# Four memsets at the front of a queue, and five queues ordered anew behind the first key products

## The chip, the cores and the metric

The kernel runs on one core of a Trainium2 chip. A core has a matrix engine (TensorE, PE in the profile; its weight loads are shown as PEld), a vector engine (VectorE, DVE), a scalar engine (ScalarE, ACT), GpSimd (POOL) and SyncE (SP), which here issues nearly all DMAs. Each engine works through its own queue in order, and the queues are tied together by semaphores. The metric is the device time of one execution in microseconds (us), the median of the runs.

## The reference

The input x has 2048 rows of 448 bf16 values. One transformer block is computed: a layer norm, linear attention with 16 heads of 28 dimensions, a residual, a second layer norm, a gated feed-forward part of width 1792, and a second residual. Cut to what matters:

```python
q, k, v = split(layernorm(x) @ wqkv)              # 16 heads of 28
phi_q = concat([softmax(q @ w_phi), softmax(-(q @ w_phi))])
phi_k = concat([softmax(k @ w_phi), softmax(-(k @ w_phi))])
kv  = einsum("bhsf,bhsd->bhfd", phi_k, v)         # sums over all 2048 rows
z   = phi_k.sum over the rows
num = einsum("bhqf,bhfd->bhqd", phi_q, kv)
den = einsum("bhqf,bhf->bhq", phi_q, z) + 1e-6
h   = x + (num / den) @ wo
g, u = layernorm(h) @ w_gate, layernorm(h) @ w_up
out = h + (sigmoid(g) * u) @ w_down
```

No query can be finished before kv and z have been summed over all rows.

## The kernel before

The 2048 rows are 16 tiles of 128 rows, numbered 0 to 15. An operation is created with a name, a list of engines that may run it, and the buffers that it reads and writes. From the buffers a class named Graph works out who has to wait for whom. The table ORDER (from line 210) is written out by hand or by a planner. It lists every operation's name in one of five queues, and so says which engine runs it and in which sequence. Nothing is reordered later: what stands behind a waiting operation waits too. The profile knows lines of the code and not names. A name is found in the trace by counting along its queue: the ninth xn of the tiles that DVE and the other engines run is xn8, and so on.

The stages and the names, with their lines:

- **First layer norm**, per tile t: x*t* loads the rows (L397); bst*t* and agg*t* are its statistics on DVE (L503, L504). For a group of tiles, ve1 and nm1 (L511, L514) prepare variance and mean, pow1 (L516, POOL alone) takes the inverse root, and nb1 (L520, POOL) the bias. The last group holds tiles 12 to 15, so ve1_12, nm1_12, pow1_12 and nb1_12 serve four tiles, and need agg15, whose rows x14 brings. xn*t* writes the normalised tile to one of three buffers (L529 on ACT, L532 on DVE or POOL). xT*t* transposes it: on PE for the first four tiles, else as a DMA issued by SP (L542). So xn8 can't start before xT5 has landed, nor xn7 before xT4.
- **Weights**: ld_k, ld_v and ld_q (L461, transposing DMAs) bring the parts of wqkv; w2m0 and w2m1 (L571) multiply them by w_phi, and w2e copies the product out of PSUM. ld_wo, ld_wg, ld_wu and ld_wd load the later weights with L397, 56 KB to 448 KB each.
- **Keys and values**, per tile: pva and pvb are the products of keys and values (L298, all paired matmuls of 64 rows share this line), ek takes both exponentials (L630, L631, ACT), ss their sums (L634, DVE), rs the reciprocals (L640, DVE), and phi the normalised features (L644; POOL for most tiles, DVE for tiles 10 and 15). phi has three buffers and ek and ss have five. v1 copies the values (L489). kva and kvb (L298) add the tile's share of kv to two PSUM banks, which seed (L666) has started with the 1e-6: a small product of two tiles epsl and epsr. These are filled by the four memsets epsl0 and epsr0 (L409, L410, L413, L414; two each), on POOL. After kvb15, kvzA to kvzD (L709 on DVE, L713 on ACT) mask the sums into a table, and kvzones puts its ones there (L434).
- **Queries**: pqa and pqb (L298) of four tiles and a quarter pair of heads, eq their exponentials (L680, L681, ACT). num*t* (L298) multiplies by the table; rsm, qq, b, c and rden (L740 to L748, DVE) combine the two halves, and o (L752, DVE or POOL) divides. oT transposes (PE for tiles 0 and 1, with the copies oT0e and oT1e, else a DMA). num*t* and num*t+1* use the same two banks: the next num waits for c of the one before.
- **Second norm**: woa and wob (L298) are the output products; h (L771 on ACT, L774 on DVE) adds the residual; nm (L777), sq (L779, ACT), ve (L782), pow2 (L784, POOL alone) and hn (L788) normalise; hT transposes (PE for tiles 0 and 1, with the copies hT0e and hT1e on DVE, else a DMA).
- **Feed-forward**: ga and gb (L298) are gate and up for a slice of 128 columns, sig (L847, ACT) and hh (L848, DVE) combine them. dn, dp, dm, dl (L298, L875) are the down products, fin (L882) the last residual, out the store. The name of a piece says the first tile and the slice: ga0_1 is slice 1 of tiles 0 and 1. Four banks serve gate and up, so a pair of slices waits for hh of the pair before.

The profile's critical chain and the queues meet in the first 80 us; from there on PE has hardly any idle time.

Of the kernel before, what the change touches and what calls it, by code (L numbers as in the profile page):

```python
# [208 lines left out]

ORDER = {  # L210
    "sp": (
        "x1 x0 ld_k0 x2 ld_k2 x4 x6 ld_v0 x10 ld_v2 x8 ld_q2 ld_q1 ld_q0 x12 ld_q3 xT4 xT5 x14 xT6 xT7 xT8 xT9 "
        "xT10 xT11 xT12 xT13 xT14 xT15 ld_wg0 ld_wu1 ld_wu3 ld_wd1 ld_wg1 ld_woe0 ld_wu0 ld_woe1 ld_woo0 ld_woo1 "
        "ld_wg3 ld_wg2 ld_wd6 ld_wd2 ld_wd3 ld_wd5 ld_wd0 ld_wu2 oT2 oT3 oT5 oT4 oT6 oT7 ld_wd4 hT3 hT2 oT8 oT9 "
        "hT4 hT5 hT6 hT7 oT11 oT10 oT12 out3 out1 hT9 hT8 oT13 hT11 hT10 oT14 oT15 out0 out5 hT12 hT14 out2 hT15 "
        "out4 hT13 out10 out7 out8 out9 out6 out11 out13 out12 out14 out15 out15b "
    ),
    "act": (
        "wphi3 wphi2 wphi1 wphi0 wTe0 wTe1 xT1e xT0e wTe2 w2e0_0 w2e0_1 w2e0_2 w2e0_3 xn3 xn4 ek0 ek1 xn5 v1_0 "
        "v1_1 xn6 ek2 v1_2 v1_3 ek3 w2e1_1 ek4 v1_4 ek5 v1_5 w2e1_0 v1_6 ek6 xn11 ek7 v1_7 xn12 ek8 xn13 ek9 "  # L220
        "w2e1_3 w2e1_2 ek10 xn14 ek11 xn15 v1_11 ek12 eq0_0 ek13 ek14 ek15 v1_14 eq0_1 kvzB eq1_0 eq1_1 eq2_0 oT0e "
        "eq2_1 h1 h0 sq1 sq0 eq3_0 eq3_1 sig0_1 sig0_0 sig0_3 sig0_2 sig0_5 sig0_4 sq2 sig0_7 sig0_6 sq3 sig0_9 "
        "sig0_8 sq5 sig0_11 sig0_10 sig0_13 sig0_12 sig2_1 sig2_0 sq4 sig2_3 sig2_2 sq7 sq6 sig2_5 sig2_4 sig2_6 "
        "sig2_7 sig2_8 sig2_9 sig2_10 sig2_11 sig2_12 sig2_13 sig4_1 sq9 sig4_0 sig4_3 sq8 sig4_2 sig4_5 sig4_4 "
        "sig4_7 sig4_6 sig4_9 sq10 sig4_8 sq11 sig4_11 sig4_10 sig4_13 sig4_12 sig8_1 sig8_0 sq13 sig8_2 sig8_3 "
        "sig8_4 sig8_5 sq12 sig8_6 sq14 sq15 sig8_7 sig8_9 sig8_8 sig8_10 sig8_11 sig8_13 sig8_12 sig12_0 sig12_1 "
        "sig12_3 sig12_2 sig12_5 sig12_4 sig12_7 sig12_6 sig12_9 sig12_8 sig12_11 sig12_10 sig12_12 sig12_13 "
    ),
    "pe": (
        "warm0 warm1 warm2 wT0 wT1 xT1 warm3 xT0 warm4 warm5 wT2 w2m0_0 wT3 warm6 w2m0_1 w2m0_2 warm7 w2m0_3 warm8 "  # L230
        "ppa0 warm9 ppb0 vva0 xT3 xT2 vvb0 ppa2 ppb2 vva2 vvb2 w2m1_1 w2m1_0 seed kva0 pva4 kvb0 pvb4 pva5 kva1 "
        "pvb5 kvb1 pva6 kva2 pvb6 pva7 w2m1_2 w2m1_3 pvb7 pva8 kvb2 kva3 pvb8 kvb3 pva9 kva4 pvb9 kvb4 pva10 kva5 "
        "pvb10 pva11 kvb5 kva6 pvb11 pqa0_0 pva12 kvb6 kva7 pvb12 kvb7 pqb0_0 kva8 pva13 kvb8 kva9 pvb13 kvb9 "
        "kva10 pva14 pvb14 kvb10 pva15 kva11 pvb15 pqa0_1 kvb11 kva12 pqb0_1 pqa1_0 kvb12 kva13 kvb13 kva14 kvb14 "
        "kva15 kvb15 pqb1_0 pqa1_1 num0 num1 pqb1_1 pqa2_0 num2 pqb2_0 pqa2_1 oT0 oT1 pqb2_1 num3 woa0 wob0 num4 "
        "pqa3_0 pqb3_0 num5 pqa3_1 pqb3_1 hT1 hT0 num6 ga0_1 ga0_0 gb0_1 gb0_0 num7 woa2 ga0_3 ga0_2 gb0_3 gb0_2 "
        "wob2 ga0_5 ga0_4 gb0_5 gb0_4 num8 woa4 ga0_7 ga0_6 gb0_7 gb0_6 wob4 num9 ga0_9 ga0_8 gb0_9 gb0_8 woa6 "
        "ga0_11 ga0_10 gb0_11 gb0_10 wob6 ga0_13 ga0_12 gb0_13 gb0_12 dn0_0 dn0_4 ga2_1 ga2_0 gb2_1 gb2_0 dn0_8 "
        "dn0_11 ga2_3 ga2_2 gb2_3 num10 gb2_2 dp0_0 dp0_4 ga2_5 ga2_4 gb2_5 gb2_4 dp0_8 dp0_11 ga2_6 ga2_7 gb2_6 "
        "gb2_7 woa8 ga2_8 ga2_9 gb2_8 gb2_9 wob8 num11 ga2_10 ga2_11 gb2_10 gb2_11 dn2_0 ga2_12 ga2_13 gb2_12 "  # L240
        "gb2_13 dn2_4 dn2_8 ga4_1 num12 gb4_1 ga4_0 dn2_11 gb4_0 dp2_0 ga4_3 ga4_2 gb4_3 dp2_4 num13 gb4_2 ga4_5 "
# [707 lines left out]
```

## Time and profile before

The median of three runs is 205.43 us (205.39 to 205.56). The profiled execution took 205.5 us, 203.7 us of them between its first and its last instruction. The TensorE clock is granted in full (1.000).

| stretch, us | PE busy | DVE busy | ACT busy | POOL busy | DMA share |
|---|---|---|---|---|---|
| 0 to 10 | 8.62 | 6.88 | 5.73 | 5.20 | 0.88 |
| 10 to 20 | 9.44 | 9.67 | 8.89 | 9.52 | 0.62 |
| 20 to 30 | 9.31 | 10.00 | 9.40 | 8.05 | 0.40 |
| 30 to 40 | 9.93 | 10.00 | 9.21 | 9.22 | 0.46 |
| 40 to 50 | 9.81 | 8.24 | 8.26 | 4.30 | 1.06 |
| 50 to 60 | 9.64 | 9.25 | 9.29 | 4.30 | 0.55 |
| 60 to 70 | 9.56 | 8.95 | 4.39 | 4.44 | 0.25 |
| 70 to 80 | 9.96 | 8.78 | 4.14 | 1.09 | 0.39 |

Busy times are microseconds out of the ten of the stretch. PE's matmuls are pipelined, so a busy PE may still be waiting inside a group; the DMA share is that of 16 DMA engines. Over the span PE is busy for 197.6 us, DVE for 135.9, ACT for 96.5 and POOL for 56.8.

### The profile page before, as it was taken

Reading aid. Unit: us, or ns where it says so; the run is one execution under the profiler, and the core shown is the slowest. Engines: PE = TensorE matmul, PEld = TensorE weight load, DVE = VectorE, ACT = ScalarE, POOL = GpSimd, SP = SyncE. Lnnn points to the kernel's source line nnn. Section 1 sums busy time; section 2 is a strip of 40 time slices with the busy share of each in tenths; the row PEclk is TensorE's granted clock in tenths of the full one; section 3 lists DMA queues with packets and bytes.
Section 4 is the critical chain, followed back from the end, with each engine's and each line's share of the span. In section 5 each row is a group of like instructions: output and inputs, shape, how many; then the busy total and the mean of one; then the engine's idle time right before and its main releaser. Section 6 shows DMA issues by size and latency. Waiting matters only on the chain.

```text
span 203.7 us, 5832 instructions
## 1 busy us (share of the span) xinstructions
PE 197.6 (97%) x2476; PEld 109.8 (54%) x2476; DVE 135.9 (67%) x329; ACT 96.5 (47%) x194; POOL 56.8 (28%) x98
## 2 busy tenths in 40 slices
PE   7999989999989999999999999999999999999995
PEld 2744545565547876777444544444555555544443
DVE  5899999988988888667667967526532422262224
ACT  2998999879893544522333343323522222222220
POOL 4599699861064320500023020001400000000000
DMA  6965332899622351230004411030212000004002
GB/s 151 318 140 122 55 80 55 245 309 345 196 52 55 65 89 28 55 81 0 3 0 80 122 29 26 3 74 24 58 40 56 3 0 3 0 0 138 0 0 90
DMA packets 32866, 16.25 MB, mean 80 GB/s; under 512 B 25096, under 2 KB 31944, under 8 KB 32840
## 3 DMA queue, kind: packets, MB, share of 16 engines
q1 hardware_dynamic: 32336, 15.86, 30.5%
q8 instruction: 19, 0.31, 0.7%
q10 hardware_dynamic: 504, 0.03, 0.2%
q14 instruction: 7, 0.06, 0.1%
HBM read 8.34 MB, written 1.84 MB: 50 GB/s over the span
## 4 chain that ended last, share of the span: by engine, by line
PE 78%; DVE 9%; POOL 4%; DMA 3%; ACT 2%; issue 1%; SPq 1%; POOLq 0%
PE psum L298 73%; PE psum L875 5%; DMA x_sb<-in_A_x_dram 3%; DVE c_sb L746 1%; DVE b_sb L743 1%; POOL rst L516 1%; DVE st L503 1%; DVE xn_pad L532 1%; DVE ss L634 1%; POOL phi L644 1%; DVE rsm L740 1%; ACT xn_pad L529 1%; SPq L397 1%; DVE o_pad L752 1%; ACT v L489 0%
## 5 line engine op out<-in xcount | busy, mean ns | idle before, releaser
L298 PE MATMUL psum<-xnT,wg_sb 64*128 64x512 bf16 (+1 forms) x490 | 93.3, 333 | 0.4 <-DVE rsm L740 0.3
L298 PE MATMUL psum<-xnT,wu_sb 64*128 64x512 bf16 (+1 forms) x490 | 93.2, 333 | 0.0
L847 ACT ACTIVATE sg_sb<-psum 128x512 bf16<-128x512 f32 (+1 forms) x70 | 35.0, 511 | 91.2 <-PE psum L298 90.7
L848 DVE SCALAR_TENSOR_TENSOR hhT<-sg_sb,psum 128x512 bf16<-128x512 bf16 (+1 forms) x70 | 38.9, 576 | 53.9 <-ACT sg_sb L847 53.2
L298 PEld LDWEIGHTS psum<-xnT,wg_sb 64*128 64x128 bf16 x490 | 44.4, 94 | 23.8 <-DVE hhT L848 4.7
L298 PEld LDWEIGHTS psum<-xnT,wu_sb 64*128 64x128 bf16 x490 | 44.4, 94 | 13.4
L298 PE MATMUL psum<-wd_sb,hhT 64*128 64x448 bf16 x336 | 36.8, 349 | 0.0
L298 PEld LDWEIGHTS psum<-wd_sb,hhT 64*128 64x128 bf16 x336 | 17.2, 94 | 15.0 <-DVE x_sb L774 0.6
L644 POOL TENSOR_TENSOR phi<-hhT,rs 128x896 bf16<-128x896 bf16 x14 | 23.3, 1688 | 2.4 <-DVE rs L640 1.9
L298 PE MATMUL psum<-Wk,xnT 64*128 64x448 bf16 x112 | 22.5, 350 | 0.5 <-ACT Wk L489 0.2
L298 PE MATMUL psum<-wv_sb,xnT 64*128 64x448 bf16 x112 | 22.5, 351 | 0.1
L782 POOL TENSOR_SCALAR ve<-ssq 128x1 f32<-128x1 f32 x14 | 3.0, 212 | 65.2 <-ACT junk L779 65.0
L634 DVE TENSOR_REDUCE ss<-hhT 128x32 f32<-128x896 bf16 x16 | 16.9, 1059 | 0.1
L298 PE MATMUL psum<-xnT,Wq 64*120 64x512 bf16 x112 | 14.7, 384 | 0.1
L298 PE MATMUL psum<-wo_o,oT 64*128 64x448 bf16 x56 | 13.2, 349 | 0.0
L298 PE MATMUL psum<-wo_e,oT 64*128 64x448 bf16 x56 | 13.1, 349 | 0.0
L875 PE MATMUL psum<-wd_sb,hhT 128*128 128x448 bf16 (+2 forms) x70 | 11.2, 316 | 0.0
L882 DVE SCALAR_TENSOR_TENSOR x_sb<-psum,x_sb 128x448 bf16<-128x448 f32 (+2 forms) x17 | 9.4, 592 | 2.2 <-PE psum L875 1.6
L779 ACT ACTIVATE junk<-x_sb,sum 128x448 bf16<-128x448 bf16 x16 | 10.5, 658 | 0.0
L503 DVE BATCH_NORM_STATS2 st<-x_sb 128x6 f32<-128x448 bf16 x16 | 9.4, 607 | 1.7 <-DMA x_sb<-in_A_x_dram 1.6
L298 PEld LDWEIGHTS psum<-Wk,xnT 64*128 64x128 bf16 x112 | 7.6, 94 | 5.4 <-PE psum L298 0.5
L746 DVE TENSOR_TENSOR c_sb<-b_sb,psum 128x464 bf16<-128x464 bf16 x16 | 10.1, 633 | 0.4
(93 smaller groups left out, 237.0 us busy)
## 6 DMA issues: line engine op xcount, KB each, us to landing
out_dram<-x_sb SPq DMA_DIRECT2D x15, 112.0 KB, 1.8
x_sb<-in_A_x_dram SPq DMA_DIRECT2D x7, 224.0 KB, 4.6
wd_sb<-in_B_w_down_dram SPq DMA_DIRECT2D x7, 224.0 KB, 9.7
wg_sb<-in_B_w_gate_dram SPq DMA_DIRECT2D x3, 448.0 KB, 8.8
wu_sb<-in_B_w_up_dram SPq DMA_DIRECT2D x3, 448.0 KB, 7.3
wv_sb<-in_A_wqkv_dram SPq DMA_DIRECT2D x2, 224.0 KB, 4.8
...
```

What stands on the lines that cost most here:

```text
L298: p = e.matmul(o, lhsT=w, rhs=r, start=st, stop=sp, tile_position=(row, 0))
L397: return op(eng, name, lambda e: e.dma_start(dst, src), r=r, w=w, dma="in" if eng == "sp" else "ain", nring=48 if eng == "sp" else 8, kb=kb)
L503: op("dve", "bst%d" % t, lambda e: e.bn_stats(st1[:, t, :], x_sb[:, t, :]), r=[("x", t)], w=[("st1", t)])
L634: op("dve", "ss%d" % t, lambda e: e.tensor_reduce(ss[:, s, :].rearrange("p (b h) -> p b h", h=2), eks.rearrange("p b (d h) -> p b h d", h= ...
L644: return e.tensor_tensor(phi[:, sp, :, :, :].rearrange("p b a n -> p (b a) n")[:, :, 0:56].rearrange("p b (d h) -> p b d h", h=2), eks.rea ...
L746: op("dve", "c%d" % t, lambda e: e.tensor_tensor(h3(c_sb), h3(b_sb), OPv[:, :, :, 0:EV], ALU.add), r=K("b") + BB, w=K("c"))
L779: op("act", "sq%d" % t, lambda e: e.activation(junk[:, t % 2, :], h_sb[:, t, :], ACT.Square, bias=sum2[:, t:t + 1], scale=-float(D), accum ...
L782: op(("pool", "dve"), "ve%d" % t, lambda e: e.tensor_scalar(ve2[:, t:t + 1], ssq2[:, t:t + 1], 1.0 / D ** 3, EPS, op0=ALU.mult, op1=ALU.ad ...
L847: op("act", "sig" + nm, lambda e: e.activation(sg_sb[:, k, 0:N], bk(bg)[:, 0:N], ACT.Tanh, scale=0.5), r=[B(bg)], w=[("sg", k)])
L848: op("dve", "hh" + nm, lambda e: e.scalar_tensor_tensor(out=hhT[(t0 // 4) % NHH][:, ff, ns], in0=sg_sb[:, k, 0:N], scalar=1.0, in1=bk(bu)[ ...
L875: p = e.matmul(bk(b)[:, lo:hi], lhsT=hb[:, ff, TS(t)], rhs=wd_sb[:, ff, lo:hi], start=ff == 0, stop=ff == FT - 1)
L882: op("dve", "fin%d%s" % (t, nm), lambda e: e.scalar_tensor_tensor(out=h_sb[:, t, lo:hi], in0=bk(b)[:, lo:hi], scalar=0.5, in1=h_sb[:, t, l ...
```

## The change

Only ORDER changes. epsl0 and epsr0 move on POOL from behind ve1_8 and v1ones to just behind wqpad, ahead of nm1_1. From the first key products on, all five queues have another sequence, up to about the place where the first down products (dn0_0) stand on PE; behind that the queues are the same. The operations, their buffers and their waits on each other are the same too. Some operations change the engine: xn5 goes from ACT to POOL; kvzones, kvzA and kvzC from DVE to ACT and kvzB from ACT to DVE; v1_15 to ACT and v1_14 to DVE; o1, o2, hn1, hn2, hn3, ve0 and ve1, nm2, nm3 and nm5 from DVE to POOL; o4, o6, o7, hn0, ve2, ve3, ve5, nm0 and nm1 from POOL to DVE; oT0e and oT1e change places; of the small group operations ve1_12, nm1_6 and nm1_8 go to POOL, and nm1_12, ve1_6 and ve1_8 to DVE. On SP, loads of later weights are put between the first loads and transposes. The core of the diff:

```diff
     "sp": (
-        "x1 x0 ld_k0 x2 ld_k2 x4 x6 ld_v0 x10 ld_v2 x8 ld_q2 ld_q1 ld_q0 x12 ld_q3 xT4 xT5 x14 xT6 xT7 xT8 xT9 "
-        "xT10 xT11 xT12 xT13 xT14 xT15 ld_wg0 ld_wu1 ld_wu3 ld_wd1 ld_wg1 ld_woe0 ld_wu0 ld_woe1 ld_woo0 ld_woo1 "
-        "ld_wg3 ld_wg2 ld_wd6 ld_wd2 ld_wd3 ld_wd5 ld_wd0 ld_wu2 oT2 oT3 oT5 oT4 oT6 oT7 ld_wd4 hT3 hT2 oT8 oT9 "
+        "x1 x0 ld_k0 x2 ld_k2 x4 x6 ld_v0 x10 ld_v2 x8 ld_woe1 ld_wu0 ld_q2 ld_q1 ld_q0 x12 ld_woo1 ld_q3 xT4 xT5 "
+        "x14 xT6 ld_wd0 xT7 xT8 ld_wd6 xT9 xT10 xT11 ld_wu2 xT12 xT13 ld_wu1 ld_wd5 xT14 xT15 ld_woo0 ld_wg0 "
+        "ld_wg1 ld_wg2 ld_wg3 ld_woe0 ld_wu3 oT3 ld_wd3 oT2 ld_wd2 oT5 oT4 oT6 ld_wd4 oT7 hT2 ld_wd1 hT3 oT8 oT9 "
...
     "act": (
-        "wphi3 wphi2 wphi1 wphi0 wTe0 wTe1 xT1e xT0e wTe2 w2e0_0 w2e0_1 w2e0_2 w2e0_3 xn3 xn4 ek0 ek1 xn5 v1_0 "
...
-        "w2e1_3 w2e1_2 ek10 xn14 ek11 xn15 v1_11 ek12 eq0_0 ek13 ek14 ek15 v1_14 eq0_1 kvzB eq1_0 eq1_1 eq2_0 oT0e "
+        "wphi3 wphi2 wphi1 wphi0 wTe0 wTe1 xT1e xT0e wTe2 w2e0_0 w2e0_1 w2e0_2 w2e0_3 xn3 xn4 ek0 ek1 v1_0 v1_1 "
...
+        "w2e1_2 w2e1_3 ek10 ek11 xn15 v1_11 ek12 eq0_0 ek13 kvzones ek14 ek15 v1_15 eq0_1 kvzA kvzC eq1_0 eq1_1 "
...
     "pe": (
...
-        "ppa0 warm9 ppb0 vva0 xT3 xT2 vvb0 ppa2 ppb2 vva2 vvb2 w2m1_1 w2m1_0 seed kva0 pva4 kvb0 pvb4 pva5 kva1 "
...
-        "kva10 pva14 pvb14 kvb10 pva15 kva11 pvb15 pqa0_1 kvb11 kva12 pqb0_1 pqa1_0 kvb12 kva13 kvb13 kva14 kvb14 "
-        "kva15 kvb15 pqb1_0 pqa1_1 num0 num1 pqb1_1 pqa2_0 num2 pqb2_0 pqa2_1 oT0 oT1 pqb2_1 num3 woa0 wob0 num4 "
-        "pqa3_0 pqb3_0 num5 pqa3_1 pqb3_1 hT1 hT0 num6 ga0_1 ga0_0 gb0_1 gb0_0 num7 woa2 ga0_3 ga0_2 gb0_3 gb0_2 "
...
+        "ppa0 warm9 ppb0 vva0 xT3 xT2 vvb0 ppa2 ppb2 vva2 vvb2 w2m1_1 seed w2m1_0 pva4 kva0 pvb4 kvb0 pva5 kva1 "
...
+        "kvb9 kva10 pvb14 kvb10 kva11 pva15 kvb11 pvb15 kva12 pqa0_1 kvb12 pqb0_1 kva13 pqa1_0 kvb13 kva14 kvb14 "
         "kva15 kvb15 pqb1_0 pqa1_1 num0 num1 pqb1_1 pqa2_0 num2 pqb2_0 pqa2_1 oT0 oT1 pqb2_1 num3 woa0 wob0 num4 "
-        "pqa3_0 pqb3_0 num5 pqa3_1 pqb3_1 hT1 hT0 num6 ga0_1 ga0_0 gb0_1 gb0_0 num7 woa2 ga0_3 ga0_2 gb0_3 gb0_2 "
+        "pqa3_0 pqb3_0 num5 pqa3_1 pqb3_1 hT1 num6 hT0 ga0_1 ga0_0 gb0_1 num7 gb0_0 woa2 ga0_3 ga0_2 gb0_3 gb0_2 "
...
     "dve": (
...
-        "bst10 agg11 bst9 bst7 agg6 agg7 agg9 bst8 agg8 agg10 mask2 xT3e xT2e ss0 nm1_8 nm1_6 rs0 ss1 bst13 rs1 "
-        "bst12 ss2 bst14 rs2 agg14 xn8 ss3 agg13 agg12 rs3 xn9 bst15 ss4 agg15 xn10 ve1_12 ss5 rs4 ss6 rs5 ss7 rs6 "
-        "v1_8 ss8 v1_9 rs7 ss9 rs8 v1_10 ss10 rs9 rs10 kvzones ss11 v1_12 rs11 phi10 ss12 v1_13 rs12 ss13 rs13 "
-        "ss14 rs14 v1_15 ss15 rs15 phi15 kvzC kvzD kvzA rsm0 qq0 rsm1 b0 qq1 c0 b1 rden0 c1 rsm2 rden1 qq2 o1 b2 "
-        "c2 oT1e rden2 rsm3 qq3 b3 c3 o2 rden3 rsm4 qq4 b4 c4 ve1 rsm5 qq5 ve0 hn1 rden4 b5 c5 hT1e hT0e rsm6 qq6 "
...
+        "bst6 bst8 mask2 agg6 agg10 agg8 agg7 bst11 ve1_6 bst9 agg11 xT3e xT2e agg9 ve1_8 ss0 rs0 ss1 bst13 bst12 "
+        "rs1 ss2 bst14 rs2 xn8 ss3 rs3 agg13 agg14 xn9 bst15 ss4 xn10 agg12 agg15 ss5 nm1_12 rs4 ss6 rs5 ss7 v1_8 "
+        "rs6 v1_9 rs7 ss8 rs8 ss9 v1_10 rs9 ss10 ss11 v1_12 rs10 rs11 phi10 ss12 rs12 v1_13 ss13 rs13 ss14 rs14 "
+        "v1_14 ss15 rs15 phi15 kvzB kvzD rsm0 qq0 rsm1 b0 qq1 c0 b1 rden0 c1 rden1 rsm2 qq2 b2 c2 oT0e rsm3 qq3 b3 "
+        "c3 rden3 rden2 rsm4 qq4 b4 c4 nm0 nm1 rsm5 qq5 b5 c5 hn0 hT1e rsm6 rden5 qq6 hT0e b6 c6 rden4 o4 rden6 "
...
     "pool": (
-        "neghalf ident0 ident phipad wqpad nm1_1 pow1_1 ve1_0 pow1_0 nm1_2 ve1_2 ve1_3 pow1_3 nm1_3 pow1_2 nb1_3 "
-        "ve1_4 nm1_4 pow1_4 nb1_4 nb1_2 xn2 opad0 ve1_6 pow1_6 ve1_8 v1ones epsl0 epsr0 pow1_8 nb1_6 phi0 nb1_8 "
-        "xn7 phi1 phi2 phi3 nm1_12 pow1_12 nb1_12 phi4 phi5 phi6 phi7 phi8 phi9 phi11 phi12 phi13 phi14 o0 nm1 o3 "
-        "pow2_1 nm0 pow2_0 hn0 o5 o4 o6 o7 ve2 pow2_2 ve3 pow2_3 ve5 ve4 pow2_4 pow2_5 ve7 pow2_7 ve6 pow2_6 ve8 "
...
+        "neghalf ident0 ident phipad wqpad epsl0 epsr0 nm1_1 pow1_1 ve1_0 pow1_0 nm1_2 ve1_2 ve1_3 pow1_3 v1ones "
+        "nm1_3 pow1_2 nb1_3 ve1_4 nm1_4 pow1_4 nb1_4 nb1_2 opad0 xn2 nm1_6 pow1_6 xn5 nm1_8 pow1_8 nb1_6 nb1_8 "
+        "phi0 xn7 phi1 phi2 phi3 ve1_12 pow1_12 nb1_12 phi4 phi5 phi6 phi7 phi8 phi9 phi11 phi12 phi13 phi14 o0 o1 "
+        "o3 o2 ve1 pow2_1 ve0 hn1 pow2_0 o5 nm2 pow2_2 nm3 pow2_3 hn2 hn3 ve4 nm5 pow2_4 pow2_5 ve7 pow2_7 ve6 "
...
```

## The prediction

> **What bounds the kernel now.** I read the page's busy shares first, then the waits and the chain, then the timelines of VectorE and GpSimd around the first wait. PE is the bound:
>
> ```profile
> PE 197.6 (97%) x2476; PEld 109.8 (54%) x2476; DVE 135.9 (67%) x329; ACT 96.5 (47%) x194; POOL 56.8 (28%) x98
> ```
>
> Its matmuls are neither more nor fewer after the change, so only PE's stalls can move. From 77 us on (dn0_0) the queues are unchanged and PE hardly waits: what it has lost or won by then stays. The waits from 14 to 30 us, and those from 46 to 62 us:
>
> ```profile
> PEld psum L298 <- POOL phi L644: 1.0, 1, 1.0
> PE psum L298 <- POOL phi L644: 0.6, 1, 0.6
> DVE st L503 <- DMA x_sb<-in_A_x_dram: 0.2, 1, 0.2
> ...
> PEld psum L298 <- DVE c_sb L746: 1.7, 4, 0.6
> PEld psum L298 <- ACT eq L681: 1.0, 3, 0.4
> ```
>
> In the first stretch PE waits once, for phi4. In the second it waits in small pieces for VectorE's c and ScalarE's eq. The chain shows why phi4 is late: x14's rows, statistics, pow1_12, nb1_12, phi4.
>
> ```profile
> 15.92 2.94 DMA x_sb<-in_A_x_dram
> ...
> 19.80 2.07 DVE xn_pad L532
> ...
> 25.56 1.04 POOL rst L516
> ...
> 26.89 1.70 POOL phi L644
> 28.59 0.05 issue
> 28.64 0.97 PE psum L298 x22
> ```
>
> And the timelines of VectorE (three lines) and GpSimd (two):
>
> ```profile
> 19.72 2.16 DVE L532 TENSOR_SCALAR xn_pad<-x_sb,nm,rst 128x512 bf16<-128x512 bf16 x1
> 23.19 0.31 DVE L532 TENSOR_SCALAR xn_pad<-x_sb,nm,rst 128x512 bf16<-128x512 bf16 x1
> 34.44 0.81 DVE L434 CAST kvz<-mask 128x24 bf16<-128x24 f32 x1
> ...
> 18.40 3.33 POOL L644 TENSOR_TENSOR phi<-hhT,rs 128x896 bf16<-128x896 bf16 x2
> 23.34 1.70 POOL L644 TENSOR_TENSOR phi<-hhT,rs 128x896 bf16<-128x896 bf16 x1 [1.62 <-DVE rs L640]
> ```
>
> xn8 (19.72) took 2.16 and ended at 21.88, just behind phi2 (end 21.72). xn9, the same work, started 0.15 ahead of phi3 and took 0.31. kvzones, 24 numbers per partition, took 0.81 and ended 0.08 behind phi8. So a VectorE instruction of these forms that meets a running phi stands still until it ends.
>
> **The change, part by part.** The profiled execution took 205.5 us (203.7 span, 1.8 around it), 0.07 over the median 205.43; durations come from it and the sum is added to the median.
>
> *Memsets.* They ran from 13.98 to 14.73, 0.75 us. In front, GpSimd is idle from 2.00 to 3.72 waiting for agg1, so they cost 0. The room goes to xn5 (0.76, until now ScalarE's at 0.83). v1ones and opad0 (0.45 and 0.35) now stand ahead of xn2 and push its end from 12.34 to about 12.7; xT2 on PE starts at 12.98, which hides it. Without that cover it would be 0.3. By the same rows phi0 starts at 15.86 (15.83 before).
>
> *Loads on SP.* ld_woe1, ld_wu0 and ld_woo1 (560 KB) now stand ahead of xT4. Their issue is three rows of about 0.47, 1.4 us. The stretches 7 to 9 us moved 374 and 384 GB/s, so the data is 1.5 us. xT4 was issued at 12.19, when xn4 was ready, behind an issue that ended at 11.66: it would go at about 13.2. xT4 itself feeds xn7 at 17.66 with 2 us to spare; x14, behind xT5, has 0. Bounds for x14's landing: 0, since the DMA share was 0.06 and 0.09 in the stretches 13 to 14 and 15 to 16 and could take the data in; +1.0, if xT4, xT5 and x14 all move with the issue. I take +0.5. The other loads moved forward (0.43 to 0.6 to issue each) stand between transposes that waited for xn, except ld_wd1, below. The 16 MB are the same, so the full DMAs of 38 to 53 us only become less full; nobody waited there.
>
> *xn8 and xn9.* The new order puts bst12 ahead of rs1, so phi1 ends at 19.9 (20.08 before), and x14 0.5 later puts rs2's end at 20.25. xn8 stands right behind rs2, phi2 needs a semaphore more: xn8 comes first and takes 0.4, a gain of 1.75. But then phi2 runs to about 22.05, when rs3 is already done (20.25 + xn8 0.35 + ss3 1.0 + rs3 0.3 = 21.9), phi3 follows without a gap, and xn9, which agg13 and agg14 now hold back by 0.16, meets it: it ends at about 23.9 instead of 23.49. The block has moved, not gone. ss4 starts at 24.3 (23.95), agg15, now behind xn10, ends at 25.8 (25.10), and the 1.84 of nm or ve, pow1_12 and nb1_12 put phi4 at 27.6 (26.89): +0.7. Bounds: -1.0 with neither blocked, +1.7 with both (x14 on time and xn9 0.16 too late).
>
> The Trainium skill, SBUF — State Buffer, Who interferes with whom, says that VectorE's two-port modes and GpSimd share one pair of ports as a lock, that whoever issues first holds it for a whole instruction, and that the other blocks fully. xn8 (2.16) and xn9 (0.31) agree; by that rule xn9 is blocked whenever phi3 goes first, and the sum is the forecast's, or with xn8 blocked as well that of the second rival.
>
> *From phi4 to kvb15.* phi4 to phi9 follow each other at 1.67: phi9 ends at 37.65 (36.91). The gaps behind it (0.44 for kvb8, 0.28 for rs12, in front of which v1_13 stood) shrink, but rs13 now comes behind v1_13 (0.53): phi10 to 38.2, ss12 and rs12 to 39.45, phi12 at 39.5, v1_13, ss13 and rs13 to 41.25, phi13 to 43.0, phi14 to 44.65, phi15 and the last pair 45.95 against 45.56: +0.4. PE saves 0.26 (pva10's wait), 0.23 (pva14 and pvb14 no longer in a row: 0.98 against 0.75) and 0.23 (kva13, kvb13); that is hidden behind the phi chain. kvzones leaves VectorE (0.68 there), which is hidden too while phi10 waits for phi9. Bounds: -1.1 and +1.7.
>
> *Masks and eq.* ScalarE had kvzB (0.60) ahead of eq1_0; now kvzA and kvzC, 1.15. eq1_0 would start 0.35 later, and pqa2_0 began 0.05 after eq1_0's end: +0.35 there. oT1 now waits for o1 on GpSimd, behind o0 (0.94): 51.95 against 51.57. num3 is 0.23 later, woa0 0.15, sq0's end 0.17, since VectorE no longer has o1 and o2 (0.66, 0.62).
>
> *hT0e.* GpSimd gets hn1 (0.77) ahead of pow2_0, which ends at 59.75 instead of 59.13; hn0, now VectorE's at 0.40, ends at 60.25 instead of 60.01. rsm6, rden5 and qq6, 0.45 by their starts, now stand ahead of hT0e: it ends at 61.35 instead of 60.92, and ga0_1 with it. This +0.43 includes the paragraph above. Bounds: 0.2, if PE fills it with num6, and 0.6.
>
> *61 to 77 us.* num9 fills the 0.20 that PE waited behind wob6 (0.77 against 0.57); num8 no longer stands ahead of woa4, and ga0_7 waits 0.12 for hh0_5: -0.08. Bounds -0.4 and +0.2.
>
> *ld_wd1.* It was issued at 37.58. Now it stands behind hT2, which waits for hn2, on GpSimd behind pow2_3: hn2 ends at 73.5, hT2's issue takes 1.2, and ld_wd4, of the same size, landed in 2.80: 77.6. All of this moves by the same 0.4 of the phi chain; dn0_0 without it would stand at 77.06 + 0.43 - 0.08 = 77.4. So +0.2; bounds 0 and +0.6. hT3 behind it lands at about 77.8 to 79.1, ga2_1 needs it at 79.
>
> Sum: 0.40 + 0.43 - 0.08 + 0.20 = +0.95: 205.43 + 0.95 = **206.4**.
>
> **Rivals.**
> 1. *Faster: neither xn is blocked.* Place: the seam between phi2 and phi3. It decides if phi2 ends before rs3's semaphore, by less than 0.15 in my times; kvzones got through such a seam, 0.06 wide, between phi8 and phi9. Then VectorE is 1.6 sooner at ss4, phi4 starts a us earlier and PE's wait (0.59 and the 0.26 behind it) goes, with the 0.46 of split pairs: kvb15 -1.1. With +0.43 - 0.08 and ld_wd1 at 0: 204.7. Against it: phi1 and phi2 left no seam for xn8.
> 2. *Slower by more: one block more.* Either x14 is not late and both xn8 and xn9 stand (+1.7 at phi4), or phi10 loses to phi11. For: before, phi10 started at 36.91, as phi9 ended, and only because phi11 still waited for kvb8 (37.20); PE now reaches kvb8 within 0.2 of phi9's end. If phi11 goes first, ss12 and all behind it wait 1.69, of which the gaps give 0.3 back: 206.4 + 1.4 = 207.8.
> 3. *No change to be told.* x14 is on time, xn9 still slips in, and PE's regained 0.7 covers eq1_0 and hT0e: 205.4. For: PE's stalls before are only 0.2 to 0.6 each. Against: hT0e's added rows lie on no cover.
>
> **Numbers.** 0.2%, 0.41 us, is about what a measurement of this kernel can tell from no change. The forecast has 0.45 (its own range 205.9 to 207.0), rival 1 0.22, rival 2 0.20, rival 3 0.13. So faster 0.22, same 0.13, slower 0.65. The range 204.8 to 207.9 leaves out about a third of rival 1 and of rival 2.
>
> **What would show it.** Four memsets ahead of 3 us. xn8 at 0.3 to 0.4 and xn9 at 1.7 to 2.1 (rival 1: both short; rival 2: both long, or phi10 starting 1.7 behind phi9). PE's wait for phi4 at 29.3. eq1_0 about 0.35 later against kvb15; hT0e behind qq6; ga0_1 near 61.9; a wait of dn0_0 for a wd load. The forecast is wrong if the x loads land as early as before, or if VectorE finds a seam at phi3.

## The result and the profile after

The changed kernel takes 207.61 us (median of 4 runs, 207.49 to 208.11) against 205.41 for the kernel before on the same chip: a ratio of 1.0123, 95% interval 1.0104 to 1.0141. Ratios here are estimates from the runs within 1.5% of the fastest of their kernel, with a 95% interval, and not quotients of the medians. The forecast was 206.4 in a range of 204.8 to 207.9. The sign was right, the size less than half. The profiled execution took 207.59 us (205.8 span), so it stands for the median.

Line numbers of the changed kernel are two higher than those of the kernel before (L298 is L300). The page's line of busy times of the changed kernel:

```profile
PE 197.2 (96%) x2476; PEld 111.8 (54%) x2476; DVE 134.0 (65%) x326; ACT 96.3 (47%) x196; POOL 57.8 (28%) x100
```

PE works as long as before (197.6) in a span that is 2.1 us longer: the loss is one or more stalls of PE. Who waited for whom between 60 and 82 us (total, times, longest):

```profile
PE psum L300 <- DMA wd_sb<-in_B_w_down_dram: 1.9, 1, 1.9
...
PE psum L300 <- DVE xnT L491: 0.9, 1, 0.9
```

The first line is new, and as long as nearly the whole loss. PE's longest wait in the same stretch before, weight loads (PEld) aside, was:

```profile
PE psum L298 <- DVE rsm L740: 0.3, 1, 0.3
```

The changed kernel's chain, in order of time (start, length, what):

```profile
45.20 0.60 ACT kvz L715 x2
45.81 0.60 ACT kvz L715 x2
46.44 1.02 ACT eq L682
...
72.27 1.52 POOL hn_pad L790 x2
73.79 0.46 SPq L797
74.29 4.59 DMA wd_sb<-in_B_w_down_dram
78.88 0.25 issue
79.13 49.61 PE psum L300 x658
```

SP stands at hT2 until hn2 is done on GpSimd (73.03), issues its transposes for 1.19 us, then ld_wd1 at 74.29. The load needs 4.59 us to land, and dn0_0 starts at 79.13 (77.06 before). The work in front of it on PE, gb0_12, starts at 76.73 in both traces. From dn0_0 on everything is 2.05 to 2.08 later, to the last matmul. So all that happens ahead of dn0_0 sums to nothing here, and ld_wd1 alone makes the loss.

What travelled while the load was on its way, by DMA queue (packets, MB, share of the engines' time) and with the median time to landing of what was issued:

```profile
q14 instruction: 1, 0.01, 2.7%
q8 instruction: 1, 0.02, 1.3%
...
wd_sb<-in_B_w_down_dram SPq DMA_DIRECT2D x1, 224.0 KB, 4.6
```

q8 brings instructions, 16,384 bytes at a time; such a packet runs about every 250 records of PE. Here it ran at 77.04, with 8,192 bytes of q14 beside it at 77.08. The load's 896-byte packets had all moved by 77.04, yet it counts as landed only at 78.88. Packets of 4 bytes, called completions here, close a transfer (16 of them this load, in the trace of e7 below). Twelve such packets started between 76.9 and 77.2 and all ended at 78.76 to 78.77, after 1.58 to 1.85 us. The profile doesn't say which of them are the load's and which are those of hT3 behind it.

The first stretch shows another order than the forecast's. Waits of the changed kernel from 14 to 30 us, then the timelines of VectorE (three lines) and GpSimd (one):

```profile
DVE st L505 <- DMA x_sb<-in_A_x_dram: 1.1, 1, 1.1
POOL phi L646 <- PE psum L300: 1.1, 1, 1.1
...
PEld psum L300 <- POOL phi L646: 0.5, 2, 0.3
```

```profile
20.14 0.63 DVE L505 BATCH_NORM_STATS2 st<-x_sb 128x6 f32<-128x448 bf16 x1 [1.11 <-DMA x_sb<-in_A_x_dram]
20.93 0.32 DVE L534 TENSOR_SCALAR xn_pad<-x_sb,nm,rst 128x512 bf16<-128x512 bf16 x1
22.65 0.38 DVE L534 TENSOR_SCALAR xn_pad<-x_sb,nm,rst 128x512 bf16<-128x512 bf16 x1
...
21.09 3.48 POOL L646 TENSOR_TENSOR phi<-hhT,rs 128x896 bf16<-128x896 bf16 x2 [1.06 <-PE psum L300]
```

x14 landed at 20.11 (18.86 before); bst14 waited 1.11 for it. xn8 (0.32, before 2.16) started while GpSimd was idle, 0.16 ahead of phi2. xn9 came up 0.14 before phi2's end at 22.79 and slipped in between phi2 and phi3. phi4 started at 26.78 (26.89), kvb15 0.40 earlier than before.

Then this was given back. Waits of the changed kernel from 46 to 62 us:

```profile
PEld psum L300 <- ACT eq L683: 1.3, 2, 1.0
...
PEld psum L300 <- DVE c_sb L748: 0.8, 2, 0.6
PE psum L300 <- ACT eq L683: 0.6, 1, 0.6
```

eq1_0 started 1.28 behind kvb15's end (0.72 before), behind kvzA and kvzC: the first three lines of the chain above. hT0e ended at 61.01 (60.92) and ga0_1 started at 61.37 (61.13), 0.24 later than before.

### The profile page after: what moved, and what is told of

The parts are those of the page before. It is cut to its first block, busy times and chain, and to the rows that moved or that the text cites. A ratio compares the mean times of both kernels' runs of the same rounds, so it can differ in the third digit from the quotient of the medians.

```text
span 205.8 us, 5832 instructions
## 1 busy us (share of the span) xinstructions
PE 197.2 (96%) x2476; PEld 111.8 (54%) x2476; DVE 134.0 (65%) x326; ACT 96.3 (47%) x196; POOL 57.8 (28%) x100
## 4 chain that ended last, share of the span: by engine, by line
PE 82%; POOL 5%; DVE 4%; DMA 3%; ACT 3%; issue 1%; SPq 0%; DVEq 0%; POOLq 0%
PE psum L300 76%; PE psum L877 5%; DMA wd_sb<-in_B_w_down_dram 2%; POOL rst L518 1%; POOL hn_pad L790 1%; DVE st L505 1%; DMA x_sb<-in_A_x_dram 1%; POOL phi L646 1%; POOL rst L786 1%; PE psum L573 1%; ACT kvz L715 1%; ACT eq L682 0%; ACT eq L683 0%; ACT hhT L633 0%; ACT hhT L632 0%
## 5 line engine op out<-in xcount | busy, mean ns | idle before, releaser
L300 PE MATMUL psum<-xnT,wg_sb 64*128 64x512 bf16 (+1 forms) x490 | 93.4, 333 | 1.0 <-DVE xnT L491 0.9
L300 PE MATMUL psum<-xnT,wu_sb 64*128 64x512 bf16 (+1 forms) x490 | 93.1, 333 | 0.0
L300 PEld LDWEIGHTS psum<-xnT,wg_sb 64*128 64x128 bf16 x490 | 44.3, 94 | 23.4 <-DVE hhT L850 4.7
L300 PEld LDWEIGHTS psum<-xnT,wu_sb 64*128 64x128 bf16 x490 | 44.3, 94 | 12.9
L300 PE MATMUL psum<-wd_sb,hhT 64*128 64x448 bf16 x336 | 36.9, 349 | 1.9 <-DMA wd_sb<-in_B_w_down_dram 1.9
L300 PEld LDWEIGHTS psum<-wd_sb,hhT 64*128 64x128 bf16 x336 | 17.6, 94 | 16.7 <-DVE hhT L850 2.1
L300 PE MATMUL psum<-Wk,xnT 64*128 64x448 bf16 x112 | 22.6, 351 | 0.7 <-ACT Wk L491 0.5
L300 PE MATMUL psum<-wv_sb,xnT 64*128 64x448 bf16 x112 | 22.7, 351 | 0.1
L300 PE MATMUL psum<-xnT,Wq 64*120 64x512 bf16 x112 | 14.9, 385 | 0.7 <-ACT eq L683 0.6
L300 PE MATMUL psum<-wo_o,oT 64*128 64x448 bf16 x56 | 13.2, 349 | 0.0
L300 PE MATMUL psum<-wo_e,oT 64*128 64x448 bf16 x56 | 13.1, 349 | 0.0
L300 PEld LDWEIGHTS psum<-Wk,xnT 64*128 64x128 bf16 x112 | 7.5, 94 | 6.6 <-ACT v L491 0.8
```

The source lines that it names most:

```text
L300: p = e.matmul(o, lhsT=w, rhs=r, start=st, stop=sp, tile_position=(row, 0))
```

## The experiments

Every time has beside it the kernel before on the same chip, 205.37 to 205.42 in the first three sets of runs, 205.59 and 205.41 in the last two; ratios are against it.

### Is ld_wd1 all of the loss?

Two kernels: the changed one with ld_wd1 early, and the one before with ld_wd1 late.

```diff
 e1_wd1_early (the changed kernel, "sp")
-... oT7 hT2 ld_wd1 hT3 ...
+... ld_wu3 ld_wd1 oT3 ...
 e2_before_wd1_late (the kernel before, "sp")
-... ld_wu3 ld_wd1 ld_wg1 ...
+... hT3 ld_wd1 hT2 ...
```

> The changed kernel with ld_wd1 alone moved back to the end of the weight loads (behind ld_wu3, issued near 41 us). Theory A: the whole loss of 2.07 us is dn0_0's wait for ld_wd1, since PE stood at 76.73 in both kernels just ahead of dn0_0. Then 205.5 us, the same as before within 0.2, and dn0_0 at 77.06. Rival B: hT3 is late next (it landed at 80.29, 0.35 ahead of ga2_1), so that a wait of ga2_1 takes the place: 206.0 to 207.0.

> The kernel before with ld_wd1 alone moved back, between hT3 and hT2. Theory A: the place of this one load costs the time by itself. hT3's issue ended at 73.91, so ld_wd1 goes at 73.95; at ld_wd4's 2.80 to landing dn0_0 (77.06) would not wait, 205.4; at the 4.59 that it took in the changed kernel it lands at 78.5 and the time is 206.9. If 205.4 comes out, the landing is not long of itself and the late issue (74.29 and behind hT2) is what counts.

e1 took 205.24 us (10 runs, ratio 1.0006, 0.9986 to 1.0026): the whole loss is gone, and with it any gain or loss of the rest that could be told. dn0_0 started at 76.62. e2 took 206.45 (ratio 1.0048, 1.0030 to 1.0067): this load alone, late, costs the kernel before 1.0 us. There it was issued at 73.98, landed after 3.93 us, and dn0_0 started at 78.16 instead of 77.06. The 0.3 us by which it was earlier and the 0.7 us by which it landed faster than in the changed kernel are the difference between the two losses.

The place in the queue decides already by one step:

```diff
 e7_wd1_ahead_hT2 (the changed kernel, "sp")
-... oT7 hT2 ld_wd1 hT3 ...
+... oT7 ld_wd1 hT2 hT3 ...
```

> The changed kernel with ld_wd1 moved by one place only, ahead of hT2 (behind oT7), instead of behind it. Theory A (the loss is that ld_wd1 stands behind hT2, which waits for hn2 until 73 us): it is issued near 71 and lands between 73.5 and 76, dn0_0 does not wait for it and starts at 76.6 to 77.1, time 205.2 to 205.5: all of the loss gone by one place. Theory B (what counts is that the load is among the last 16-engine transfers at 75 to 77 us, where packets stand for 1 to 1.8 us; wherever it stands late, something needed behind it pays): dn0_0 or the ga2 products wait for it or for hT2, hT3, time 206 or more.

205.37 us (ratio 1.0000, 0.9985 to 1.0015). Theory A: the load went out at 70.60, since it no longer waited for hn2, and had landed at 73.34.

```profile
q1 hardware_dynamic: 820, 0.36, 47.6%
...
wd_sb<-in_B_w_down_dram SPq DMA_DIRECT2D x1, 224.0 KB, 2.7
```

These are the queues and the load between 70.5 and 73.4 us of that kernel. No instruction packet ran, and the load landed in 2.74.

### Why did the load take 4.59 us to land?

First suspect: hT3's transposes, which follow it and whose 256-byte packets stood together with those completions.

```diff
 e10_hT3_behind_oT8 (the changed kernel, "sp")
-... hT2 ld_wd1 hT3 oT8 oT9 ...
+... hT2 ld_wd1 oT8 hT3 oT9 ...
```

> The changed kernel with nothing but hT3's transposes moved from behind ld_wd1 to behind oT8, so that ld_wd1 still waits behind hT2 but shares the DMA engines with no transpose that follows it. Read at ld_wd1 and dn0_0, not at the end time, since hT3 now comes late for ga2_1 (it should land near 81.5, some 2.5 us after ga2_1 needs it). Theory A (the last 1.6 to 1.8 us of ld_wd1's landing belong to hT3's transposes, whose small packets stood together with the load's): it lands in 2.7 to 3.0 instead of 4.59, that is near 77.2, and dn0_0 starts at 77.2 to 77.5 instead of 79.13. Theory B (they belong to the load itself, or to the 16 KB instruction fetch that ran at 77.0): it lands after 4.3 to 4.7 again and dn0_0 starts at 78.8 to 79.2.

The load took 4.38 us with no transpose behind it before oT8 was issued at 78.70; dn0_0 started at 79.72, 0.24 behind the landing. (The end, 209.61 us, is later still because hT3 came late, as meant.) So it isn't hT3. The queues of this kernel from 75 to 79.5 us:

```profile
GB/s 73 243 291 282 232 43 1 0 0 0 0 24 64 104 72 225 215 327 358 303 263 88 16 73 0 0 8 8 8 8 16 8 8 16 24 24 0 0 0 0
...
q8 instruction: 1, 0.02, 1.8%
q14 instruction: 1, 0.01, 0.7%
...
wd_sb<-in_B_w_down_dram SPq DMA_DIRECT2D x1, 224.0 KB, 4.4
```

The row of GB/s has 40 slices of 0.11 us. The bulk of the load is through by 77.6; a thin tail of 8 to 24 GB/s follows until 79.1. In the packets this tail is 16 of the load's 256, and the 16 KB instruction packet had run from 76.71 to 78.02. That suggested the fetch. Over the 24 late loads of this size in the traces taken (ld_wd4 and ld_wd1), the landing sorts by it:

| a 16 KB instruction packet | loads | time to landing, us |
|---|---|---|
| none between issue and landing | 10 | 2.71 to 2.87; once 3.26, beside an 8 KB packet (e16, below); beside another one (e3) 2.86 |
| running when the load was issued | 3 | 3.38 to 3.59 |
| began between issue and landing | 11 | 3.69 to 4.73 |

Of the eleven, only ld_wd1 in the changed kernel and in e10 had an 8 KB packet beside it as well, so that packet doesn't make the difference. A coincidence in time is not yet a cause, so the fetch was moved, with all orders left alone: more and shorter warm-up matmuls on zeros at the head of PE's queue let it come so many instructions earlier.

```diff
 e14_fetch_moved_away (the changed kernel), e15_wd1_ahead_fetch_into (e7)
-for i, (n, size) in enumerate(((9, 512), (1, 128), ...
+for i, (n, size) in enumerate(((89, 32), (1, 128), ...
```

> The changed kernel, its orders as they are, with warm0 as 89 matmuls of 32 columns on zeros instead of 9 of 512, so that TensorE's queue has 160 instructions more (80 matmuls, 80 weight loads) ahead of all else and its 16,384-byte instruction fetch, which came at 77.04 on the changed kernel's trace, comes about 160 instructions earlier in the order: by the trace at 72.8 to 73.9, ahead of ld_wd1's packets. Theory A (the fetch shares a DMA engine with the load and holds that engine's rows and what queues behind them): ld_wd1 lands in 2.7 to 3.4 instead of 4.59, dn0_0 starts at 77.1 to 77.6 instead of 79.13, time 205.6 to 206.0 instead of 207.6, which is the loss the forecast had for this term. Theory B (the landing is long for another reason, such as being queued behind hT2's transposes, and the fetch only happened beside it): 4.3 to 4.7 again, dn0_0 at 79, time 207.5.

> The seventh experiment (ld_wd1 ahead of hT2, landed in 2.74, 205.37) with the same 80 matmuls more in warm0. The fetch that came at 75.81 there should come near 71.5 to 72.5, among ld_wd1's packets (71.75 to 73.0 there). Theory A: ld_wd1 now lands in 3.7 to 4.7, at 74.3 to 75.3, still ahead of dn0_0, so the time stays within 0.3 of 205.4; that also prices the added matmuls themselves, which stand in the first 6 us, at nothing. Theory B: 2.7 to 2.9 as before. If the time moves by more than 0.3 the added matmuls cost something of their own, and the time of the run beside this one has to be read less that.

Both landings moved the way theory A has it. In e14 the load was issued at 74.94 behind the same hT2, and these are the queues from 74.9 to 77.9 us:

```profile
q1 hardware_dynamic: 1351, 0.49, 71.8%
...
wd_sb<-in_B_w_down_dram SPq DMA_DIRECT2D x1, 224.0 KB, 2.9
```

2.87 instead of 4.59. In e15 the fetch ran at 72.47, as the load was issued (72.62), and it took 3.59 instead of 2.74, 0.74 of these 0.85 in its issue (1.31 instead of 0.57). That a fetch lengthens the time from issue to landing is therefore shown in both directions. But the time of e14 did not fall: 208.32 us (ratio 1.0144, 1.0114 to 1.0173). The fetch came at 71.35, earlier than expected, onto oT7's transposes. The queues of e14 from 70.2 to 74.5 us, and what PE waited for from 70 to 80:

```profile
q8 instruction: 1, 0.02, 2.3%
...
oT<-o_pad SPq DMA_TRANSPOSE x1, 4.1
```

```profile
PEld psum L300 <- DMA oT<-o_pad: 1.6, 1, 1.6
PE psum L300 <- DMA oT<-o_pad: 1.3, 1, 1.3
```

oT7 landed after 4.14 us (2.31 in the changed kernel), woa6 waited for it, and dn0_0 started at 79.07 though the load had been there since 77.81. e15 took 208.19 (ratio 1.0143), 2.8 us above e7: its fetch held oT7 too (landed 75.06), and its kvb15 was 2.0 later, 0.8 of it already at phi4. So the added matmuls are not free, as that expectation had allowed for, and the end times of e14 and e15 don't price the fetch alone. A third place was tried:

```diff
 e16_fetch_between (the changed kernel)
-for i, (n, size) in enumerate(((9, 512), (1, 128), ...
+for i, (n, size) in enumerate(((57, 80), (1, 128), ...
```

> The changed kernel, its orders as they are, with warm0 as 57 matmuls of 80 columns (about as many columns as 9 of 512): 96 instructions more on TensorE instead of the 160 of the fourteenth kernel, so that the fetch should fall between two transfers that TensorE waits for, behind oT7 (landed 71.94 on the changed kernel's trace) and ahead of ld_wd1's packets (75.5 to 77.0), at 72.5 to 74.5. Theory A (the whole loss of the changed kernel is that a fetch meets a transfer which lands last before TensorE needs it): ld_wd1 lands in 2.7 to 3.4, woa6 does not wait for oT7, dn0_0 starts at 77.1 to 77.7, time 205.6 to 206.2, with not one instruction in another order. Theory B (there is always something late enough to be hit in this order, or the landing is not the cause of the loss): dn0_0 at 78.5 to 79.2, time 207 or more.

208.5 us (206.4 to 210.56, ratio 1.0108, 1.0072 to 1.0144): theory B, with dn0_0 at 80.33, later than either theory had it. The profile is of the run of 208.75. The fetch came at 75.07 and met hT2. SP's timeline of this kernel:

```profile
74.67 2.11 SPq L797 DMA_TRANSPOSE xnT<-hn_pad  x1
76.82 0.58 SPq L399 DMA_DIRECT2D wd_sb<-in_B_w_down_dram  x1
```

The transposes' issue took 2.11 instead of 1.19, and ld_wd1 behind it landed at 80.08. In this profile xn9 was held as well (1.34 us); phi4 came 0.8 later and kvb15 1.8. What is shown, then: where the added matmuls moved the fetch onto a transfer, its landing grew by 0.85 (the load in e15) to 1.8 us (oT7 in e14). That the changed order with the fetch between all late transfers would run at 205.7 is not shown; in this order oT7, hT2 and ld_wd1 follow each other so closely that each place tried hit one of them.

### The front of GpSimd's queue, and VectorE's seams

The memsets alone:

```diff
 e3_memsets_only (the kernel before, "pool")
-neghalf ident0 ident phipad wqpad nm1_1 ... v1ones epsl0 epsr0 pow1_8 ...
+neghalf ident0 ident phipad wqpad epsl0 epsr0 nm1_1 ... v1ones pow1_8 ...
```

> The kernel before with only the four memsets of epsl and epsr moved to the front of GpSimd's queue. Theory A: hidden in 1.72 us of idle time, and what stands behind them at 14 us is hidden by rs0 (15.33): 205.4, no difference above 0.2 us. Rival: GpSimd's pow1_8, nb1_6 and xn6 come 0.7 sooner and bring phi0 and phi1 forward: 204.9.

204.71 us (10 runs, 204.51 to 205.08; ratio 0.9972, 0.9961 to 0.9984): faster by 0.28%, and the best kernel of this study. Its timelines, VectorE in two lines and GpSimd in one:

```profile
19.76 0.38 DVE L532 TENSOR_SCALAR xn_pad<-x_sb,nm,rst 128x512 bf16<-128x512 bf16 x1
...
21.44 0.39 DVE L532 TENSOR_SCALAR xn_pad<-x_sb,nm,rst 128x512 bf16<-128x512 bf16 x1
...
18.05 5.32 POOL L644 TENSOR_TENSOR phi<-hhT,rs 128x896 bf16<-128x896 bf16 x3
```

phi0 and phi1 run 0.34 earlier, so that phi1 ends (19.74) as xn8 comes up, and not 0.36 after it. xn8 passes in the 0.14 between phi1 and phi2; xn9 comes up 0.24 before phi2's end and passes at its seam with phi3, which follows without a gap. The phi behind takes 1.73 to 1.80 instead of 1.69. phi4 starts at 25.25 (26.89) and kvb15 at 44.47 (45.27). Being in step with the seams is worth 1.6 us to GpSimd and 0.8 to PE, whose own work takes over from kva4.

Putting xn9 past the seam measures the block itself:

```diff
 e6_xn9_behind_bst15 (e1, "dve")
-... agg14 xn9 bst15 ss4 ...
+... agg14 bst15 xn9 ss4 ...
```

> The changed kernel with ld_wd1 early, and xn9 moved behind bst15 on VectorE, so that phi3 has been running for 0.5 us when xn9 comes up. Theory A (a running phi shuts out an xn until it ends; only a seam lets it in): xn9 takes 1.2 to 1.6 instead of 0.38 and ends with phi3 at 23.8, ss4 starts 1.0 later (bst15 being done already), phi4 at 27.2 instead of 26.1, kvb15 0.8 to 1.1 later, time 206.1. Theory B (xn9 is not shut out by phi3, the 0.31 and 0.38 are its ordinary time whatever GpSimd does, and xn8's 2.16 had another cause): xn9 takes 0.4, nothing moves, 205.2.

206.0 us (ratio 1.0049, 1.0030 to 1.0068), 0.76 above e1: theory A. VectorE's xn9 and GpSimd's phi1 to phi3:

```profile
22.53 1.43 DVE L532 TENSOR_SCALAR xn_pad<-x_sb,nm,rst 128x512 bf16<-128x512 bf16 x1
...
18.69 5.12 POOL L644 TENSOR_TENSOR phi<-hhT,rs 128x896 bf16<-128x896 bf16 x3
```

It ended at 23.96, with phi3 at 23.81. phi4 came 1.09 later, kvb15 0.74. Undoing the early loads, the other thing that moved xn8, did little:

```diff
 e5_loads_back (e1, "sp")
-... x8 ld_woe1 ld_wu0 ld_q2 ld_q1 ld_q0 x12 ld_woo1 ld_q3 ...
+... x8 ld_q2 ld_q1 ld_q0 x12 ld_q3 ... xT15 ld_woe1 ld_wu0 ld_woo1 ld_woo0 ...
```

> The changed kernel with ld_wd1 early (as in the first experiment, 205.24) and with the loads ld_woe1, ld_wu0, ld_woo1 back in their old place behind the transposes of the wave. Theory A (the early loads delay x14 by 0.6 to 1.25 us, and that delay is paid in phase 1, more in some runs than in others because the issue of ld_q3 takes 1.1 to 2.3 us): x14 lands at 18.9 instead of 19.4 to 20.1, xn8 and xn9 take 0.3 to 0.4, phi4 starts near 25.3 instead of 26.1 to 26.8, kvb15 near 44.0, time 204.7, and its runs lie within 0.6 us of each other instead of 1.6. Theory B (PE is the bound from kva4 on, x14's delay is covered): kvb15 stays at 44.4, time 205.2. Theory C (with x14 early xn8 meets phi2 again): xn8 takes 2.1, phi4 starts at 26.9, kvb15 at 45.3, time 205.9.

205.14 us (204.77 to 205.49), 0.1 below e1: theory B for the time. x14 landed at 18.84, 0.58 earlier than in e1, but xn8 came only 0.19 earlier, phi4 at 26.04 (26.09) and kvb15 at 44.59 (44.42). GpSimd was not level in the two profiles: phi1 ended 0.32 later in e5. So this run doesn't price the delay of x14 by itself. The runs do lie closer together than e1's (204.81 to 206.42), as theory A had it.

### Masks, hT0e, num8 and num9

```diff
 e4_wd1_early_kvz (e1)
-"act": ... eq0_1 kvzA kvzC eq1_0 ...   "dve": ... phi15 kvzB kvzD rsm0 ...
+"act": ... eq0_1 kvzB eq1_0 ...        "dve": ... phi15 kvzC kvzD kvzA rsm0 ...
 e13_memsets_masks (e3): the same edit the other way round
```

> The changed kernel with ld_wd1 early as in the first run and the four mask operations on their engines of before (kvzC, kvzD, kvzA on VectorE, kvzB on ScalarE). Theory A: eq1_0 starts 0.56 us sooner (0.72 behind kvb15's end instead of 1.28), pqa2_0 with it, and 0.3 to 0.5 of that reaches the end, since PE, VectorE and ScalarE hand on to each other from there: 205.0 to 205.2, against 205.5 without. Rival: the next waits (num3 for c2, oT1 for o1) take it up: 205.5.

> The kernel before with the memsets in front and, of the changed orders, only the masks' engines: kvzA and kvzC on ScalarE, kvzB on VectorE. Theory A (the longer row of masks on ScalarE holds eq1_0, and PE pays it): eq1_0 starts 1.28 behind kvb15's end instead of 0.72, pqa2_0 0.35 to 0.55 later, ga0_1 0.3 later, time 205.0. Theory B (PE's small waits for c and eq behind it take it up, as the equal medians of the first and fourth experiments, 205.24 and 205.33, say): ga0_1 within 0.1 of 60.34, time 204.7.

e4: 205.33 (ratio 1.0000), level with e1 within their scatter, though its profile shows eq1_0 at 0.72 behind kvb15 again and ga0_1 0.36 earlier (0.22 of it already at kvb15). On the quieter e3 the same edit is clearer: e13 took 204.97 (ratio 0.9987), 0.26 above e3. eq1_0 started 1.27 behind kvb15's end. Counted from kvb15, pqa2_0 is 0.56 later, num5 0.22 and ga0_1 0.21. So PE takes up more than half of it.

```diff
 e9_masks_hT0e_back (e4)
-"pool": ... ve0 hn1 pow2_0 o5 ...  "dve": ... c5 hn0 hT1e rsm6 rden5 qq6 hT0e b6 ...
+"pool": ... ve0 pow2_0 hn0 o5 ...  "dve": ... c5 hn1 hT1e hT0e rsm6 rden5 qq6 b6 ...
 e12_memsets_hT0e_late (e3)
-"pool": ... nm0 pow2_0 hn0 o5 ...  "dve": ... ve0 hn1 rden4 b5 c5 hT1e hT0e rsm6 qq6 rden5 b6 ...
+"pool": ... nm0 hn1 pow2_0 o5 ...  "dve": ... ve0 rden4 b5 c5 hn0 hT1e rsm6 qq6 rden5 hT0e b6 ...
```

> The changed kernel with ld_wd1 early, the masks back on their old engines (as in the fourth experiment, 205.33), and hT0e back ahead of rsm6 with hn0 on GpSimd and hn1 on VectorE as before. Theory A (the rows put ahead of hT0e are paid at ga0_1): hT0e ends 0.4 earlier against num5 than in the fourth experiment (3.1 instead of 3.5 behind num5's end), ga0_1 near 60.2, and the time is 0.3 to 0.4 lower, 204.9 to 205.0. Theory B (PE fills the gap with num6, or what follows waits for sig or hh instead): ga0_1 as early, but dn0_0 no earlier than 0.1 against num5; time 205.3.

> The kernel before with the memsets in front and, of the changed orders, only the work ahead of hT0e: hn1 on GpSimd ahead of pow2_0, hn0 on VectorE, and hT0e behind rsm6, qq6 and rden5. Theory A (what stands ahead of pow2_0 and hT0e is paid at ga0_1, the forecast's +0.43 less the masks' share): hn0 ends 0.4 later, ga0_1 at 60.7 to 60.8 instead of 60.34, dn0_0 0.3 to 0.4 later, time 205.05. Theory B (PE fills the time with num6 and catches up, the forecast's lower bound): ga0_1 at 60.5, time 204.8. Theory C (hn0 on VectorE runs free of GpSimd and takes 0.40 instead of 0.77, so nothing is lost): 204.7.

e9 went the wrong way: 206.49 (ratio 1.0051, 1.0033 to 1.0069), neither theory. Its profile is of the fastest run, 205.79. hn1, back on VectorE, stood behind c5 (58.27 to 58.91) and met GpSimd's hn0, which had started at 58.42. VectorE's hn1, an instruction of the same form as an xn, and GpSimd's hn0 in e9:

```profile
58.83 0.51 DVE L788 TENSOR_SCALAR hn_pad<-x_sb,nm,rst 128x512 bf16<-128x512 bf16 x1
...
58.42 0.77 POOL L788 TENSOR_SCALAR hn_pad<-x_sb,nm,rst 128x512 bf16<-128x512 bf16 x1
```

hn1 ended at 59.34, 0.14 behind hn0, where e4 had 58.36, on GpSimd; ga0_1 was 0.56 later. Of these 0.98 most is the place behind c5; the meeting with hn0 is worth about 0.1 (0.51, against 0.41 for hn0 on VectorE in e4). e12, the edit from the other side, took 205.56 (ratio 1.0024, 1.0003 to 1.0045), 0.85 above e3: the loss of theory A and more, but not by a later hn0. VectorE's qq6 and hT0e:

```profile
60.22 0.17 DVE L741 TENSOR_TENSOR qq<-rsm,psum 128x16 f32<-128x16 f32 x1
...
60.47 0.36 DVE L489 COPY xnT<-psum 128x512 bf16<-128x512 bf16 x1
```

hn0 was done at 59.09, 0.13 earlier than in e3. hT0e stood behind qq6, which waited for num6, and started at 60.47 instead of 59.71; ga0_1 was 0.69 later, 0.81 counted from kvb15.

```diff
 e11_memsets_num8_num9 (e3, "pe"; rsm8 qq8 b8 c8 and rsm9 qq9 moved as far on "dve")
-... num8 woa4 ga0_7 ga0_6 gb0_7 gb0_6 wob4 num9 ga0_9 ... wob6 ga0_13 ...
+... woa4 ga0_7 ga0_6 gb0_7 gb0_6 num8 wob4 ga0_9 ... wob6 num9 ga0_13 ...
```

> The kernel before with the memsets in front (as in the third experiment, 204.71) and, of the changed orders, only num8 behind gb0_6 and num9 behind wob6 on TensorE, with their rsm, qq, b, c rows moved as far on VectorE. Theory A (num9 fills PE's wait behind wob6, and woa4 and ga0_7 lose theirs: the term of -0.08, which the trace of the changed kernel showed as -0.24): ga0_1 to dn0_0 takes 15.7 instead of 15.92, time 204.5. Theory B (the wait moves on to hh0_12 and hh0_13, which dn0_0 needs): 15.9, time 204.7.

205.03 (ratio 0.9988): no gain, 0.32 above e3. ga0_1 to dn0_0 took 16.03, theory B. In this profile hT2's issue took 2.64, and PE waited 0.3 for a transpose behind dn0_0.

## Why the prediction was right and wrong

**"Loads on SP", x14 0.5 late: the size was off.** It landed 1.25 later, past the bound of 1.0, since ld_q3's issue took 2.33 (1.12 before). That too goes with an instruction packet: one ran from 12.57 to 14.18, inside this issue. In e14 and e16, which move the fetch ahead of it, the issue took 1.27 and 1.25; in e6, e7 and e9 the packet came behind it, the issue took 1.25 to 1.27, and x14 landed 0.6 to 0.8 later than before, near the forecast. (A packet that began in the last 0.4 us of the issue, in the kernel before, did nothing.) That a late x14 is paid at phi4 was right: in the changed kernel, e1, e4, e7 and e9 phi4 starts 6.66 to 6.67 behind x14's landing (7.17 in e10). How much of it reaches the end is open (e5).

**"xn8 and xn9": half right, and the sign of its term wrong.** xn8 was free, as forecast. "It meets it" failed: xn9 was not held by phi3 but came through the seam between phi2 and phi3, the place of the first rival; "if VectorE finds a seam at phi3" was the prediction's own sign of being wrong. That a running phi blocks an xn was right: e6 restored a block, with 1.43 us for xn9 and 1.09 at phi4, where the bounds for none and one block lie 1.7 apart.

**"From phi4 to kvb15: +0.4": measured -0.40**, because it stood on that block: phi4 was 0.11 earlier instead of 0.7 later, and the 0.3 that the forecast won behind phi4 came out (0.29). This is one trace; with the same order up to there kvb15 ended 1.08 earlier (e4) to 0.41 later (e10) than before. phi10 and the chain behind it kept their order, so nothing of the second rival happened.

**The memsets' 0 holds in the changed order only.** There xn5 takes their room and phi1 ends at 20.03 (20.08 before). The text gave the idle start of the queue as its reason and counted nothing for the place they left; alone, that place is worth 0.7 us (e3).

**"Masks and eq" with "hT0e": +0.43 forecast, +0.64 measured** between kvb15 and ga0_1 (-0.40 to +0.24), just past the upper bound of 0.6. Alone, on e3, and counted from kvb15, the masks cost ga0_1 0.21 and the rows ahead of hT0e 0.81. The two don't add in the changed kernel. There num6 runs ahead of hT0 (59.67 and 60.03), so qq6 waits less for it, which would explain that; it was not tried alone.

**"61 to 77 us: -0.08": measured -0.24** (ga0_1 +0.24, gb0_12 0.00). e11 found no gain in num8 and num9 by themselves.

**"ld_wd1: +0.20, bounds 0 and +0.6": measured +2.07, and this is where the forecast failed.** The mechanism stood in it: the load behind hT2, hT2 behind hn2, "a wait of dn0_0 for a wd load". The issue was even 0.5 earlier than its working had it. The step that failed is "ld_wd4, of the same size, landed in 2.80": ld_wd1 took 4.59. The 2.80 was one landing, of a load that met no fetch. These are the queues of the kernel before while that load was on its way (69.7 to 72.6 us), with no line of instructions:

```profile
q1 hardware_dynamic: 393, 0.25, 34.6%
...
wd_sb<-in_B_w_down_dram SPq DMA_DIRECT2D x1, 224.0 KB, 2.8
```

Of the 24 late loads 11 met one and took 3.69 to 4.73. The trace of before already had the price, in its queues from 74.05 to 77.9 us:

```profile
q8 instruction: 1, 0.02, 2.3%
...
xnT<-hn_pad SPq DMA_TRANSPOSE x1, 3.7
```

That is hT2, which landed in 3.74 us (hT3 in 2.29) beside a fetch that started at 75.03, just where ld_wd1 was going to travel. With those 1.45 added, 4.25 instead of 2.80, the bound would have stood near +1.6. The other terms' errors (0.8 too slow at kvb15) left the sum right in sign and wrong in its reasons. That the time fell inside the range is luck: it was that wide for other mishaps (one more block of VectorE), and this one had not been priced.
